# Full-height matmuls, shared memory regions with early loads, packed norms and prepared tail loads in a kernel of two attention halves

## Chip, cores, metric

The kernel runs on one core of a Trainium2 chip. The metric is the device time of one execution in microseconds (us), the median of several runs; executions of one kernel mostly agree within about 0.3%. "Span" is the length of the one execution that the profiler recorded.

The engines: PE (TensorE, matrix multiplies; PEld are its weight loads), DVE (VectorE), ACT (ScalarE), POOL (GpSimd, called PoolE in the prediction) and SP, which here only issues DMAs. "SPq" and "ACTq" in the profile are DMAs issued by SP and ACT. L459 is line 459 of the kernel file.

## The reference

One sequence of S = 2048 rows, D = 448 columns, H = 16 heads of 28. Half A is linear attention, half B is softmax attention with one shared key and value head. Outputs are the forward result of both halves, side by side, and the gradients of both inputs and all weights.

```python
# half A                                      phi(t) = where(t > 0, t + 1, exp(t)) + 1e-6
q, k, v = heads(x @ wqkv);  pq, pk = phi(q), phi(k)
kv  = einsum("bhsd,bhse->bhde", pk, v);  z = einsum("bhsd->bhd", pk)
num = einsum("bhqd,bhde->bhqe", pq, kv)
den = einsum("bhqd,bhd->bhq", pq, z)[..., None] + 1e-6
a   = join(num / den) @ wo
# half B
q = heads(x @ wq);  k = x @ wk;  v = x @ wv                   # k and v: one head of 28
p = softmax(einsum("bhqd,bkd->bhqk", q, k) * 28 ** -0.5)
b = join(einsum("bhqk,bkd->bhqd", p, v)) @ wo
out = concatenate([a, b]);  gradients = vjp(out)(grad_out)
```

D = 448 is three chunks of 128 and one of 64. A contraction over D is therefore a group of four matmuls, the last of which has only 64 rows.

## The kernel before

Cut to what the change and the argument touch; `...` marks cuts. `nc.sync` issues a DMA from SP, `nc.scalar` from ACT. Tiles of a pool with `bufs=3` share three buffers: the fourth user waits for the release of the first.

```python
DC_ROWS = [128, 128, 128, 64]
# --- half A: start and projection
xa = load_nat(cA, Ax2, "xa", nc.sync)                     # four loads
for q4 in range(4): dma_T(xaT, xa, 4 * q4, 4)             # DMA transposes, sync queue
def proj(st, off):
    ps = gen([P, D])
    for c in range(4):
        r = DC_ROWS[c]
        mm(ps[:, :], xaT[0:r, st, c, :], w3[0:r, c, off:off + D], start=(c == 0), stop=(c == 3))
    return ps
def phi(ps, dst, eng):
    E = awk.tile([P, D], F32, name="phiE")
    nc.scalar.activation(out=E[:], in_=ps[:, :], func=ACT.Exp)
    eng.tensor_scalar(out=E[:], in0=E[:], scalar1=1.0, scalar2=1e-6, op0=ALU.min, op1=ALU.add)
    nc.vector.scalar_tensor_tensor(out=dst, in0=ps[:, :], scalar=0.0, in1=E[:], op0=ALU.max, op1=ALU.add)
# --- q stage: 16 x phi(proj(st, 0), pq[...], nc.gpsimd), then the denominators
for q4 in range(4):
    ...                                                   # den = pq^T @ Zm, rden = 1 / den on DVE
    for s in range(4):
        nc.vector.tensor_scalar(out=wq_n[...], in0=pq[...], ...)
        nc.gpsimd.tensor_tensor(out=wd, in0=wd, in1=rb, op=ALU.mult)      # group "wdq" of the profile
        nc.vector.tensor_tensor(out=pv, in0=pv, in1=rb, op=ALU.mult)
...
# --- A's last stage: gradient of A's x
for st in range(NS):                                      # NS = 16 row blocks
    ps = gen([P, D])
    for tT_, w_ in [(gqT, wqT), (pkT, VWT), (gkT, wkT)]:
        for k in range(4):
            mm(ps[:, :], tT_[0:DC_ROWS[k], st, k, :], w_[0:DC_ROWS[k], k, :], ...)
    ot = awk.tile([P, D], BF16, name="osb")               # one of three buffers
    nc.any.tensor_copy(out=ot[:], in_=ps[:, :])           # ACT, here
    nc.scalar.dma_start(out1[st * P:(st + 1) * P, :], ot[:])
pa.close()                                                # all of A's memory is given back
# --- half B begins with its loads, on the sync queue
...
# --- norms: softmax is shifted by |q| * max|k|, one row per head in qT
for g in range(4):
    for qc in range(NQC):
        qs = bwk.tile([P, 512], F32, name="qsq")
        nc.vector.tensor_tensor(out=qs[:], in0=qT_B[g][...], in1=qT_B[g][...], op=ALU.mult)
        mm(ps[:, :], bsel[:, :], qs[:, :])
        for j in range(4):
            nc.scalar.activation(out=qT_B[g][32 * j:32 * j + 1, ...], in_=ps[32 * j:32 * j + 1, :],
                                 func=ACT.Sqrt, scale=kmax2_bc[32 * j:32 * j + 1, 0:1])
# --- core: 540 hand-ordered steps, not changed
# --- tail: weights, x and grad_out of B are loaded again; woB_pr in 16 loads, wqB_pad in pieces of 28 columns
woB_pr = load_wo_padrows(t4, B_wo, "woB_pr2")
wqB_pad = load_w_pad(t4, B_wq, 0, "wqB_pad2")
```

## Time and profile before

1429.03 us, median of three runs (1428.99 to 1429.32). The recorded execution has a span of 1425.0 us.

The first view is the table of windows. Each line is a stretch of the span in us, its length, the busy time of each engine with the number of instructions, the granted share of TensorE's full clock, the mean busy share of the DMA engines and what they moved. The stretches are: the q stage, A's last stage, the wait for B's loads, the norms, the steady part of the core, the wait for the tail's loads.

```profile
core 0: us, PE busy (x) PEld busy (x) DVE busy (x) ACT busy (x) POOL busy (x), PEclk, DMA share, GB/s
55.10:120.90 65.80, 54.57 (x267) 23.23 (x266) 40.96 (x74) 13.21 (x25) 47.24 (x32) 0.77 0.45 76
...
250.00:297.50 47.50, 46.37 (x193) 14.52 (x192) 1.15 (x3) 9.38 (x18) 0.00 (x0) 1.00 0.14 45
297.50:336.40 38.90, 6.62 (x49) 4.83 (x49) 6.66 (x44) 0.00 (x0) 7.84 (x16) 0.52 0.93 177
...
410.00:464.20 54.20, 31.84 (x38) 8.39 (x39) 15.42 (x22) 44.69 (x65) 0.00 (x0) 0.58 0.00 0
490.00:1305.40 815.40, 788.88 (x13334) 290.60 (x13327) 734.17 (x1336) 781.08 (x1561) 643.76 (x699) 0.99 1.05 174
1305.40:1340.90 35.50, 6.66 (x85) 3.40 (x84) 2.67 (x12) 3.40 (x8) 3.75 (x7) 0.60 0.81 187
```

No single engine bounds the kernel: each stretch has its own limit. PE bounds A's last stage, the DMAs the two waits, ACT the norms. The core is full on PE and ACT and is not touched.

The second view is the timeline of one group of four matmuls in A's last stage (start in us, busy us, engine, line, operation, shapes, count; in brackets the idle time before and what ended it). A weight load of 64 rows (256.42) is followed by the next group's first load and matmul only 0.29 us later (256.71), where full loads let matmuls start 0.19 us apart; groups start 0.97 us apart (256.71, 257.68).

```profile
256.42 0.09 PEld L94 LDWEIGHTS <-pqpT 64*128 64x128 bf16 x1 [0.37 <-issue]
256.71 0.30 PEld L94 LDWEIGHTS <-pq 128*128 128x128 bf16 x3 [0.20 <-issue]
256.71 1.04 PE L94 MATMUL agen<-KO,pq 128*128 128x448 bf16 x4
...
257.68 1.03 PE L94 MATMUL agen<-ga,gaT 128*128 128x448 bf16 x4
```

The timeline of the norms and of the core's entry: sixteen activations of one row of 512 cost 11.08 us, 0.69 each, and there are 64.

```profile
419.81 11.08 ACT L685 ACTIVATE qT_B_2018<-ps_qn,kmax_bc 1x512 bf16<-1x512 f32 x16 [0.19 <-PE ps_qn L94]
...
464.95 1.28 ACT L756 ACT_TABLE_LOAD   x1 [0.78 <-ACT qT_B_2021 L685]
466.25 0.60 ACT L756 ACTIVATE eT<-sps 128x512 bf16<-128x512 f32 x1
```

POOL's waits in the q stage (engine, line and tile, what it waited for, us in total, times, longest). With 47.24 of 65.8 us busy, POOL is idle almost only in these waits.

```profile
POOL phiE L338 <- ACT phiE L337: 9.9, 2, 5.7
POOL wdq L431 <- DVE rden L423: 6.0, 2, 4.7
```

### The profile page before, as it was taken

Reading aid. Unit: us, or ns where it says so; the run is one execution under the profiler, and the core shown is the slowest. Engines: PE = TensorE matmul, PEld = TensorE weight load, DVE = VectorE, ACT = ScalarE, POOL = GpSimd, SP = SyncE. Lnnn points to the kernel's source line nnn. Section 1 sums busy time; section 2 is a strip of 40 time slices with the busy share of each in tenths; the row PEclk is TensorE's granted clock in tenths of the full one; section 3 lists DMA queues with packets and bytes.
Section 4 is the critical chain, followed back from the end, with each engine's and each line's share of the span. In section 5 each row is a group of like instructions: output and inputs, shape, how many; then the busy total and the mean of one; then the engine's idle time right before and its main releaser. Section 6 shows DMA issues by size and latency. Waiting matters only on the chain. (4 is left out here: it accounts for less than half of the span.)

```text
span 1425.0 us, 39198 instructions
## 1 busy us (share of the span) xinstructions
PE 1261.8 (89%) x15698; PEld 473.9 (33%) x15706; DVE 896.3 (63%) x1707; ACT 961.8 (67%) x1880; POOL 768.4 (54%) x828
## 2 busy tenths in 40 slices
PE   3989979946985999999999999999999999997499
PEld 1333333311321233333333333333333333332353
DVE  1558520010131389899898998889989998886210
ACT  1321201202449899999999999999999999993123
POOL 5363070020300277778777777777777787776000
PEclk9979978967985589999999999999999999999599
DMA  9435813156200899999999998999999999994511
GB/s 250 87 58 106 166 26 67 47 126 106 67 23 0 155 159 168 176 185 168 184 190 168 187 183 164 184 185 177 179 188 160 191 187 172 194 168 134 89 52 64
DMA packets 675878, 197.33 MB, mean 138 GB/s; under 512 B 640464, under 2 KB 671152, under 8 KB 675696
## 3 DMA queue, kind: packets, MB, share of 16 engines
q1 hardware_dynamic: 665840, 186.07, 75.7%
q10 hardware_dynamic: 9728, 8.72, 2.0%
q8 instruction: 123, 2.02, 0.5%
q14 instruction: 59, 0.48, 0.1%
q0 software_dynamic: 128, 0.05, 0.0%
HBM read 24.81 MB, written 13.99 MB: 27 GB/s over the span
## 5 line engine op out<-in xcount | busy, mean ns | idle before, releaser
L764 POOL TENSOR_TENSOR dsT<-cp,eT 128x512 bf16<-128x512 bf16 x512 | 590.7, 1154 | 178.7 <-ACT cp L763 139.7
L761 DVE TENSOR_TENSOR dsT<-dps,eT 128x512 bf16<-128x512 f32 x512 | 348.6, 681 | 60.7 <-PE dps L708 34.8
L877 DVE STREAM_TRANSPOSE dsx<-dsT 128x512 f32<-128x512 f32 x512 | 358.0, 699 | 1.0
L756 ACT ACTIVATE eT<-sps 128x512 bf16<-128x512 f32 x512 | 307.8, 601 | 21.6 <-PE dps L708 15.3
L763 ACT ACTIVATE cp<-dps 128x512 bf16<-128x512 f32 x512 | 305.6, 597 | 10.3 <-PE dps L708 10.2
L766 ACT ACTIVATE eT<-sps 128x512 bf16<-128x512 f32 x512 | 312.1, 610 | 0.0
L708 PE MATMUL dk_acc<-dsx,qX 32*32 32x512 bf16 x4096 | 289.7, 377 | 0.4 <-DVE dsx L877 0.4
L708 PE MATMUL dps<-doT,vT_rep 32*128 32x256 bf16 x2048 | 262.3, 274 | 7.0 <-ACT cp L763 0.4
L708 PE MATMUL oq<-eT,vaug 128*32 128x256 bf16 x2048 | 218.1, 283 | 0.6
L708 PE MATMUL oq<-dsT,kn 128*32 128x256 bf16 x2048 | 204.0, 280 | 0.3
L708 PEld LDWEIGHTS <-kT_rep 32*128 32x128 bf16 x2048 | 90.6, 91 | 194.9 <-issue 157.1
L708 PEld LDWEIGHTS <-vaug 128*32 128x32 bf16 x2048 | 68.0, 94 | 189.9 <-issue 189.3
L708 PEld LDWEIGHTS <-qX 32*32 32x32 bf16 x4096 | 70.3, 89 | 93.4 <-issue 52.5
L708 PEld LDWEIGHTS <-vT_rep 32*128 32x128 bf16 x2048 | 85.9, 91 | 20.6 <-issue 19.9
L708 PE MATMUL dv_acc<-eN,don 128*32 128x512 bf16 x1024 | 86.7, 387 | 0.0
L708 PE MATMUL sps<-qT_B_2018,kT_rep 32*128 32x256 bf16 x512 | 65.5, 291 | 11.5 <-ACT qT_B_2021 L685 9.0
L708 PE MATMUL sps<-qT_B_2019,kT_rep 32*128 32x256 bf16 x512 | 65.4, 286 | 0.9 <-ACT eT L766 0.2
L794 POOL TENSOR_TENSOR don<-do_nat,rl 128x128 bf16<-128x128 bf16 x64 | 25.7, 402 | 71.0 <-DVE rl L786 71.0
L708 PE MATMUL sps<-qT_B_2021,kT_rep 32*128 32x256 bf16 x512 | 62.3, 276 | 0.8
L708 PE MATMUL sps<-qT_B_2020,kT_rep 32*128 32x256 bf16 x512 | 62.1, 276 | 0.8
L527 POOL TENSOR_SCALAR osb<-pk 128x448 bf16<-128x448 bf16 x16 | 27.3, 1706 | 65.8 <-ACT osb L511 64.6
L708 PEld LDWEIGHTS <-kn 128*32 128x32 bf16 x2048 | 58.5, 94 | 12.3 <-issue 6.4
(392 smaller groups left out, 1386.5 us busy)
## 6 DMA issues: line engine op xcount, KB each, us to landing
qX<-qn_d SPq DMA_DIRECT2D x128, 64.0 KB
out_dram<-osb ACTq DMA_DIRECT2D x44, 112.0 KB
eN<-eT SPq DMA_TRANSPOSE x256
xb_nat<-in_B_x_dram SPq DMA_DIRECT2D x2, 1792.0 KB
qn_d<-qn_sb SPq DMA_DIRECT2D x16, 128.0 KB
on_d<-onat SPq DMA_DIRECT2D x8, 256.0 KB
onat_B<-on_d SPq DMA_DIRECT2D x1, 2048.0 KB
xa<-in_A_x_dram SPq DMA_DIRECT2D x4, 448.0 KB
```

The lines of the kernel that those rows point to most:

```text
L527: nc.gpsimd.tensor_scalar(out=dph[:], in0=pk[:, st, 0:D], scalar1=-1e-6, scalar2=1.0, op0=ALU.add, op1=ALU.min)
L708: nc.tensor.matmul(out, lhsT=lhsT, rhs=rhs, start=start, stop=stop, tile_position=pos, skip_group_check=True)
L756: nc.scalar.activation(out=et[:, u % 2, 0, :], in_=sp[0][:, :], func=ACT.Exp, scale=scale)
L761: nc.vector.tensor_tensor(out=dst[:, 0, :], in0=dp[0][:, :], in1=ew[:, w % 2, 0, :], op=ALU.mult)
L763: nc.scalar.activation(out=cp[:, :], in_=dp[1][:, :], func=ACT.Copy)
L764: nc.gpsimd.tensor_tensor(out=dst[:, 1, :], in0=cp[:, :], in1=ew[:, w % 2, 1, :], op=ALU.mult)
L766: nc.scalar.activation(out=et[:, u % 2, 1, :], in_=sp[1][:, :], func=ACT.Exp, scale=scale)
L794: nc.gpsimd.tensor_tensor(out=dn[:], in0=dnv, in1=r_[:].to_broadcast([P, 2, 2, 32]), op=ALU.mult)
L877: nc.vector.transpose(out=dsx[b][:, tp, :, :, :].rearrange("p h t c -> p (h t c)").bitcast(F32), in_=dsT[y][:, :, :].rearrange("p h c -> p ...
```

## The change

Its intent has four parts. Matmuls outside the core get full 128-row operands, padded with zeros. A and B share three large memory regions, so that B's loads and transposes can be issued inside A. The norms pack 16 heads into one 16-row sum. The tail loads prepared weights and uses DMA transposes. Along with this the start loads x in eight pieces on two queues and transposes it on PE, the denominators move between the q projections, and all of A's stores move from ACT's queue to SP's. The diff is cut to its core.

```diff
-            for c in range(4):
-                r = DC_ROWS[c]
-                mm(ps[:, :], xaT[0:r, st, c, :], w3[0:r, c, off:off + D], ...)
+            for c in range(4):
+                mm(ps[:, :], xaT[:, st, c, :], w3[:, c, off:off + D], ...)      # likewise in all of A and B-pre
...
+    R1 = reg.tile([P, 4, S], BF16, name="R1")          # A: tT, gqn;  B: qT
+    R2 = reg.tile([P, NS, 512], BF16, name="R2")       # A: xaT;      B: do_nat
+    R3 = reg.tile([P, 4, 1408], BF16, name="R3")       # A: w3;       B: kT, vT, vaug, kn
...
+        qs = [nc.sync, nc.scalar]
+        for i in range(8):
+            qs[i % 2].dma_start(xa[:, 2 * i:2 * i + 2, 0:D], ...)
+        def xT(st): ...                                # PE transposes in place of dma_T(xaT, xa, ...)
...
+        qproj(0) ... qproj(1) ... den(0); qproj(2) ... den(1); qproj(3); den(2)      # den(3) in A's loop
...
+        xb = pk                                        # inside A: pk is free after gkn
+        load_nat(xb, Bx2, nc.sync)
...                                                     # loads of B's wq, wk, wv, wo and their spreading
+        for q4 in range(4): dma_T(xbT, xb, 4 * q4, 4)
+        ...                                            # woTp, wo_d, gb, wqTt, wqT_d, all on the sync queue
         for st in range(NS):                           # A's last stage
...
-            nc.scalar.dma_start(out1[st * P:(st + 1) * P, :], ot[:])
+            nc.sync.dma_start(out1[st * P:(st + 1) * P, :], ot[:])
...
+        for qc in range(NQC):
+            pn = gen([P, 512])
+            for g in range(4):
+                ...                                    # qT[:, g, ...] by projection, sq = qT * qT in bf16
+                mm(pn[:, :], bsel[:, g, :], sq[:, :], start=(g == 0), stop=(g == 3))
+            nc.scalar.activation(out=shift[:, ...], in_=pn[0:H, :], func=ACT.Sqrt, scale=kmax2[:, 0:1])
+        for g in range(4): nc.sync.dma_start_transpose(qn[:, :, g * P:(g + 1) * P], qT[:, g, :])
+        for h in range(H): nc.sync.dma_start(qT[32 * j:32 * j + 1, g, :], shift[h:h + 1, :])
+        nc.sync.dma_start(qn_d[:, :]..., qn[:, :, :])
...
+        for w in range(2):                             # last in B-pre: wk, wv transposed for the tail
+            wt = awk.tile([P, 512], BF16, name="osb")[:, 0:D]
+            for c in range(4): nc.sync.dma_start_transpose(wt[...], rep[0:r, w, c, :])
+            nc.sync.dma_start(wkvT_d[32 * w:32 * w + 32, :], wt[0:32, :])
```

## The prediction

> **What bounds the kernel now** (busy time per window). Half A runs to 297.5 us. PE waits for B's loads until 336.4 (busy 6.6 of 38.9). B's projections last to 410 (PE busy 72 of 74), norms to 464 (ACT busy 45 of 54, clock 0.58). The core lasts 841 us, ScalarE busy 781 of its last 815. PE then waits for reloads until 1341; the tail ends at 1425. The change touches everything but the core, 584 us. In the new order PE, VectorE and ScalarE run the core's instructions in the same order: 841 again, plus or minus 5.
>
> **Padding.** In the timeline full 128-row matmuls start 0.19 us apart. A 64-row load is not hidden: into and out of it the step is 0.29. A group of four costs 0.96 instead of 0.76. The Trainium skill (TensorE: Matmul & The Clock Gate, Part 2) says loads are pulled ahead if row groups do not conflict or the background buffer takes them; this trace agrees only for full loads. A's last stage (48 groups) falls from 47.5 to 37; B's projections lose 24 times 0.2 and, as natural-layout q becomes DMA transposes, 16 groups of 1.06.
>
> **Stage by stage**
> - Start: the first matmul (22.8) waits for A's x, whole, and its DMA transposes. Smaller loads, two queues, PE transposes: about 8. PE step 1.73 becomes 1.9. Worth 11.
> - q stage (57 to 121): PoolE is the bottleneck, 16 x 1.71 + 16 x 1.28 = 48 us, spread over 63. The denominators move into it. Worth 15.
> - A's loop: 2.96 becomes 2.6 per row block. Worth 7.
> - Rest of A: VW stays PoolE-bound (16 x 1.7). Padding worth 15, 10 of it in the last stage. A ends near 250.
> - B's load wait, 39: gone, hidden behind A's last stage.
> - B's projections and norms, 128: PE work about 47. The 64 one-row square roots of 0.69 (44 us) become 4. New chain on the sync queue after the last q copy: 4 transposes (2.7 each), 16 one-row shift writes (0.5), a 2 MB write (10), 8 small transposes (1.3), two small writes. The first exp waits for the release of A's pool, therefore for all these: 36 us after q. Core starts 64 after A ends, near 315 instead of 464.
> - Tail: 119.5 from the core's end. The reload stays: 3.9 MB before gwo at 187 GB/s (the rate there now) is 21 us, then 2.7 MB and 8 transposes of 2.7. PE order puts out-projection behind transposes, so PE waits 10, and again for dq. PE work falls from 78 to 60. About 97. Worth 22.
>
> Sum: 150 before the core, 22 after. **Predicted 1257 us, 80% range 1228 to 1290.** Faster by over 2%: 0.97; within 2%: 0.02; slower: 0.01.
>
> **What would show it:** first matmul near 8; A's end near 250; first exp near 315, released by a DMA of the sync queue; core 841; core end to finish 97, PE waiting for DMA transposes in it; no step of 0.29 in padded stages.
>
> **What would make it wrong:** A's stores are now on the sync queue, in order behind transposes and B's loads; a blocked store fills three output buffers and stops PE (5 to 20 slower). DMA transposes slower than 2.7 at the core's entry or in the tail (10 to 25). VectorE slowed beside PoolE (0.61 became 1.36 for one multiply). New waits in the core: small.

## The result, and the profile after

1260.73 us, median of four runs (1259.38 to 1261.30), against 1429.01 of the kernel before in the same rounds. The ratio is 0.8826, with a 95% interval of 0.8810 to 0.8843. A ratio here is always the mean time of one kernel's fast runs over the mean of the other's fast runs of the same rounds, so it is not quite the ratio of the medians quoted.

The total was predicted within 4 us. The stages were not. Boundaries are read from both timelines; gains are before minus after, in us.

| stage | before | after | gain | predicted gain |
|---|---|---|---|---|
| start and k stage, to the first phi on POOL | 55.1 | 44.5 | 10.6 | 11 |
| q stage | 65.8 | 65.8 | 0 | 15 |
| A's loop | 44.9 | 35.9 | 9.0 | 7 |
| rest of A before its last stage | 84.2 | 73.4 | 10.8 | 5 |
| A's last stage | 47.5 | 49.8 | -2.3 | 10 |
| wait for B's loads | 38.9 | 0 | 38.9 | 39 |
| B's projections and norms, to the first exp | 129.9 | 69.3 | 60.6 | 63 to 64 |
| core, first exp to the end | 839.2 | 836.7 | 2.5 | 0 |
| tail | 119.5 | 84.3 | 35.2 | 22 |

The gains sum to 165.3; the two spans (1425.0 and 1259.6) differ by 165.4, the rest is rounding. The first exp came at 338.65, not near 315, and the tail took 84.3, not 97: two errors of opposite sign.

The windows after: the q stage, A's last stage, the stretch from the last q copy to the first exp, the steady part of the core, the tail, and the first 10 us of the tail:

```profile
core 0: us, PE busy (x) PEld busy (x) DVE busy (x) ACT busy (x) POOL busy (x), PEclk, DMA share, GB/s
44.50:110.30 65.80, 43.47 (x275) 21.40 (x273) 42.49 (x78) 12.19 (x23) 47.36 (x32) 0.84 0.47 77
...
219.50:269.40 49.90, 39.07 (x195) 19.49 (x193) 0.57 (x1) 8.81 (x18) 2.02 (x17) 0.86 0.79 185
...
300.50:338.70 38.20, 21.31 (x211) 11.30 (x213) 3.06 (x6) 13.66 (x23) 0.17 (x1) 0.84 0.57 120
364.00:1175.30 811.30, 785.46 (x13318) 289.71 (x13314) 732.15 (x1332) 779.29 (x1558) 642.19 (x697) 1.00 1.08 176
1175.30:1259.60 84.30, 66.96 (x412) 32.26 (x416) 12.38 (x22) 17.04 (x35) 3.16 (x3) 0.89 0.73 184
1175.30:1185.30 10.00, 4.63 (x80) 2.55 (x81) 3.65 (x8) 2.73 (x5) 3.16 (x3) 0.90 0.93 301
```

In A's last stage PE's work fell from 46.4 to 39.1 us, as intended, but the stage did not shrink. The timeline there shows why:

```profile
238.41 5.37 SPq L101 DMA_TRANSPOSE kv<-K_154  x4
243.88 1.50 SPq L460 DMA_DIRECT2D out_dram<-osb  x3
...
245.87 1.49 ACT L459 CAST osb<-agen 128x448 bf16<-128x448 f32 x3 [17.04 <-DMA out_dram<-osb]
246.45 1.65 PE L79 MATMUL agen<-KO,pq 128*128 128x448 bf16 x4 [10.83 <-ACT osb L459]
...
247.90 1.70 PE L79 MATMUL agen<-ga,pqpT 128*128 128x448 bf16 x4
...
252.70 0.92 PE L79 MATMUL agen<-ga,gaT 128*128 128x448 bf16 x4
...
253.45 0.73 PE L79 MATMUL agen<-KO,pq 128*128 128x448 bf16 x3
```

Read it backwards. PE stood still for 10.83 us until ACT copied a result out of PSUM (L459). ACT had waited 17.04 us for a store that had to free one of three output buffers. The stage's first three stores (L460) were not issued before 243.88, behind transposes for B on the same queue, although the stage began at 219.56. Afterwards PE runs at half speed for about 4 us: groups start 1.45 to 1.5 us apart (246.45, 247.90, 249.39) instead of 0.76 (252.70, 253.45). The Trainium skill (TensorE: Matmul & The Clock Gate, Part 1) says that an idle window of about 3.4 us halves PE's clock, and a busy one restores it; this trace agrees: after the 10.83 us without work the granted clock was 0.50 from 246.45 to 250.88, and the steps are full again from 251.94 on.

POOL's waits in the q stage after: the sum (3.7 + 12.0 = 15.7) is that of before (9.9 + 6.0 = 15.9).

```profile
POOL phiE L205 <- ACT phiE L204: 3.7, 1, 3.7
POOL wdq L281 <- DVE rden L273: 12.0, 4, 5.0
```

The core's entry. The last q copy is done at 300.47. Four transposes (10.46 us) and 16 shift rows (10.08 us) follow on the sync queue, then:

```profile
321.21 0.58 SPq L521 DMA_DIRECT2D qn_d<-pk  x1
321.89 13.97 SPq L538 DMA_TRANSPOSE osb<-K_155  x8
...
336.03 1.39 SPq L539 DMA_DIRECT2D wkvT_d<-osb  x2
337.36 1.28 ACT L624 ACT_TABLE_LOAD   x1 [14.74 <-DMA osb<-K_155]
...
338.65 0.60 ACT L624 ACTIVATE eT<-sps 128x512 bf16<-128x512 f32 x1
```

ACT waits for the eight small transposes, which the core itself does not need: they hold memory that the core's first tiles reuse. In the tail the gradient of wo starts 10.0 us after the core's end (1175.33), where the prediction had counted 21:

```profile
1185.34 4.98 PE L79 MATMUL pacc<-gb_24528,onat_B 128*128 128x448 bf16 x13 [2.87 <-DMA gb_24528<-in_grad_out_dram]
```

### The profile page after: what moved, and what is told of

It reads as the page before. It is cut to its first block, busy times and chain, and to the rows that moved or that the text cites. A ratio compares the mean times of both kernels' runs of the same rounds, so it can differ in the third digit from the quotient of the medians.

```text
span 1259.6 us, 38409 instructions
## 1 busy us (share of the span) xinstructions
PE 1136.0 (90%) x15382; PEld 457.1 (36%) x15388; DVE 876.8 (70%) x1601; ACT 904.9 (72%) x1788; POOL 781.1 (62%) x861
## 4 chain that ended last, share of the span: by engine, by line
PE 56%; ACT 20%; issue 8%; POOL 5%; DVE 4%; SPq 4%; DMA 2%; ACTq 0%; POOLq 0%; DVEq 0%
PE dk_acc L576 15%; PE oq L576 10%; PE agen L79 10%; ACT eT L634 9%; ACT cp L631 9%; PE sps L576 7%; PE dps L576 5%; PE dv_acc L576 2%; PE aacc L79 2%; POOL osb L383 2%; PE pgen L79 2%; POOL phiE L205 2%; PE sps L690 1%; SPq L87 1%; PE pacc L79 1%
## 5 line engine op out<-in xcount | busy, mean ns | idle before, releaser
L576 PEld LDWEIGHTS <-R_65 32*128 32x128 bf16 (+1 forms) x8192 | 174.3, 93 | 420.8 <-issue 375.7
L631 ACT ACTIVATE cp<-dps 128x512 bf16<-128x512 f32 x512 | 305.4, 596 | 10.2 <-PE dps L576 10.1
L576 PE MATMUL sps<-R_63,R_65 32*128 32x256 bf16 x2048 | 254.0, 281 | 19.9 <-ACT eT L624 16.2
L576 PE MATMUL dps<-doT,R_65 32*128 32x256 bf16 x2048 | 261.2, 273 | 7.0 <-DVE dsT L629 0.3
L576 PE MATMUL oq<-eT,R_65 128*32 128x256 bf16 x2048 | 218.1, 283 | 0.5
L576 PE MATMUL oq<-dsT,R_65 128*32 128x256 bf16 x2048 | 203.7, 279 | 0.3 <-ACT R_63 L739 0.2
L736 DVE COPY oTs<-oq 64x256 f32<-64x256 f32 x64 | 26.7, 417 | 59.3 <-ACT eT L624 39.8
L662 POOL TENSOR_TENSOR don<-R_64,rl 128x128 bf16<-128x128 bf16 x64 | 25.8, 403 | 42.5 <-DMA eN<-eT 42.5
L205 POOL TENSOR_SCALAR phiE<-phiE 128x448 f32<-128x448 f32 x16 | 27.3, 1706 | 20.5 <-DVE zrow L230 15.7
L79 PE MATMUL agen<-R_65,R_64 128*128 128x448 bf16 x128 | 33.2, 405 | 6.2 <-ACT R_64 L192 4.5
L576 PEld LDWEIGHTS <-don 128*32 128x32 bf16 x1024 | 34.8, 98 | 0.5
```

The lines of the kernel that those rows point to most:

```text
L79: nc.tensor.matmul(out_ap, lhsT=lhsT, rhs=rhs, start=start, stop=stop, tile_position=(0, 0))
L576: nc.tensor.matmul(out, lhsT=lhsT, rhs=rhs, start=start, stop=stop, tile_position=pos, skip_group_check=True)
L631: nc.scalar.activation(out=cp[:, :], in_=dp[1][:, :], func=ACT.Copy)
L662: nc.gpsimd.tensor_tensor(out=dn[:], in0=dnv, in1=r_[:].to_broadcast([P, 2, 2, 32]), op=ALU.mult)
L736: nc.vector.tensor_copy(out=oTs[v // 8][:, :], in_=oq[0:64, 0:256])
```

## The experiments

Twelve kernels were run, each timed in three rounds, each with the right result. Times are medians; "after" is 1260.73. Each group shared the runs of the kernel before (medians 1426.8 to 1429.5). The kernel after the change was timed in other rounds than these runs, so a difference to it in us is rough: by the ratios, experiments 1 and 2 and the two runs of experiment 3 give -8.3, -13.4, +4.7 and -2.7 us instead of the -8.9, -14.8, +3.2 and -3.1 below. The interval of the change is 0.8810 to 0.8843; where a run's interval overlaps it, as in both runs of experiment 3, the time decides nothing. Each run has one trace.

| run | us | ratio to before, 95% |
|---|---|---|
| stores of A's last stage on ACT's queue | 1251.88 | 0.8768 (0.8750 to 0.8787) |
| q's phi on VectorE | 1245.95 | 0.8732 (0.8713 to 0.8751) |
| wk and wv transposes early | 1263.94 | 0.8859 (0.8838 to 0.8880) |
| the same, own buffers | 1257.65 | 0.8807 (0.8790 to 0.8823) |
| padding undone | 1287.28 | 0.9014 (0.8992 to 0.9035) |
| before with compact norms alone | 1400.33 | 0.9807 (0.9793 to 0.9822) |
| before with a wide load of wq in the tail | 1424.20 | 0.9982 (0.9958 to 1.0005) |
| B's loads later in the program | 1255.33 | 0.8792 (0.8775 to 0.8810) |
| x of B forced late, stores on ACT's queue | 1258.51 | 0.8810 (0.8795 to 0.8824) |
| four repairs | 1234.48 | 0.8643 (0.8628 to 0.8659) |
| four repairs, tail's stores on ACT's queue | 1235.96 | 0.8646 (0.8623 to 0.8669) |
| four repairs, transposes kept out of the stores | 1230.78 | 0.8621 (0.8592 to 0.8650) |

### 1. Which queue holds the stores

```diff
-            nc.sync.dma_start(out1[st * P:(st + 1) * P, :], ot[:])
+            nc.scalar.dma_start(out1[st * P:(st + 1) * P, :], ot[:])
```

> Edit: after the change, with the sixteen stores of A's last stage back on the ScalarE queue, as they were before the change. Theory (blocked store queue): the stall of 10.8 us of PE at 246, released by an eviction that waited for a store, is made by the sync queue, on which the stores stand behind B's transposes and loads; the last stage, 49.6 us, falls to 36 to 39 us and the time by 9 to 13 us, to 1248 to 1252. Rival (DMA engines are full there, whoever issues): the stall moves or stays, the last stage stays above 46 us and the time falls by less than 4 us.

Measured: 1251.88, 8.9 us less. The window of the last stage in this run:

```profile
core 0: us, PE busy (x) PEld busy (x) DVE busy (x) ACT busy (x) POOL busy (x), PEclk, DMA share, GB/s
220.80:258.90 38.10, 36.60 (x195) 18.83 (x193) 0.57 (x1) 8.76 (x18) 2.02 (x17) 1.00 1.10 226
```

The stage takes 38.0 us from its first group (220.87) to the first projection of B (258.85), at full clock, and the DMA engines move 226 GB/s instead of 185. The engines were not full; the queue was blocked. The rival falls. The predicted length of the stage, 37, is nearly reached once the store queue is repaired.

The Trainium skill (DMA: Bandwidth & Descriptors, Issuing engines are not separate DMA queues) says that starting DMAs from several engines only saves the time of issuing, which is usually small. Here it was not small. The issue of the sixteen stores themselves takes 0.34 to 0.49 us each. But on the shared queue the first three stood behind other DMAs, whose records fill 14.2 of the 14.9 us from 229.01 to 243.88, and moving the stores bought 8.9 us. The skill's page Perfetto Trace Analysis (DMA Optimizations, separating input and output engines) gives the advice that fits, and this run agrees with it.

### 2. What bounds the q stage

```diff
-                phi(proj(st, 0), pq[:, st, 0:D], nc.gpsimd)
+                phi(proj(st, 0), pq[:, st, 0:D], nc.vector)
```

> Edit: after the change, with the min-add step of phi in the q stage on VectorE instead of PoolE (16 instructions of 1.71 us leave PoolE). Theory (the q stage is bound by PoolE): the stage, 42.9 to 110.3, gets 12 to 20 us shorter, the time falls to 1241 to 1249. Rival (the stage is bound by the chain of DMA transposes, denominators and reciprocals, or by VectorE): the stage keeps 63 us or more and the time falls by less than 5 us, or rises.

Measured: 1245.95, 14.8 us less. The stage from the first phi to the loop:

```profile
core 0: us, PE busy (x) PEld busy (x) DVE busy (x) ACT busy (x) POOL busy (x), PEclk, DMA share, GB/s
45.00:96.90 51.90, 39.52 (x276) 20.27 (x275) 46.89 (x94) 12.20 (x25) 20.08 (x16) 0.93 0.56 97
```

POOL lost 27.3 us of work, VectorE gained 4.4, and the stage shrank by 13.9. So POOL's work was on the path, and the theory stands; but half of the 27 us was not returned, so POOL was not the only limit. The same instruction (min and add on 128x448 fp32) takes 1.71 us on POOL and 0.39 on VectorE (in the k stage before; in this run 0.38 at the median and up to 1.13). The Trainium skill (GPSIMD Engine Reference, 4.1 Engine selection) calls GpSimd roughly line-rate for one input; here it is 4.3 times slower than VectorE.

### 3. What holds the core's first exp

The block that transposes wk and wv was moved from the end of B's preparation to its start.

```diff
+        for w in range(2): ...                 # moved here, ahead of B's projections
         for qc in range(NQC):
             for w, dst in [(0, kT), (1, vT)]:
...
-        for w in range(2): ...                 # was last in phase_B_pre
```

> Edit: after the change, with the eight small transposes and two writes of B's wk and wv (for the tail) issued before B's projections instead of after the 2 MB write of q. Theory (the first exp waits for the release of A's pool, which these transposes hold): the first exp moves from 338.7 to between 323 and 329 and the time falls by 8 to 14 us, to 1247 to 1253. Rival (the first exp waits for the write of q, the shift rows or ScalarE's table load, whichever comes last anyway): the first exp stays after 334 and the time falls by less than 4 us.

Measured: 1263.94, 3.2 us more, which is not clear of noise. The theory seemed to fall. The timeline shows what was overlooked:

```profile
272.28 10.05 SPq L478 DMA_TRANSPOSE osb<-K  x8
...
284.16 0.41 DVE L496 TENSOR_TENSOR osb<-R 32x512 bf16<-32x512 bf16 x1 [9.87 <-DMA wkvT_d<-osb]
...
338.01 1.28 ACT L624 ACT_TABLE_LOAD   x1 [6.46 <-DMA qn_d<-pk]
```

The moved transposes took two of the three buffers named osb, and the k norms, which use the same buffers, waited 9.87 us for them. q came 8.9 us later (first transpose of q at 309.40 instead of 300.47), while the way from there to the first exp shrank from 38.2 to 29.9 us. The next run took the buffers out of the picture.

```diff
-            wt = awk.tile([P, 512], BF16, name="osb")[:, 0:D]
+            wt = pqr[:, 5 + w, 0:D]
```

> Edit: as the run before that moved the eight small transposes of wk and wv ahead of B's projections, but with a place of their own (free columns of pq) in place of two of the three shared output buffers. There the k norms waited for those buffers, q came 9 us later (first transpose of q at 309.4 against 300.5), and the way from there to the first exp shrank from 38.2 to 29.9 us. Theory (the late transposes hold the release of A's pool): q comes again near 300, the first exp near 330, the time falls by 6 to 10 us, to 1251 to 1255. Rival (something else delayed q in that run, or the norms gain only because they came late): the first exp stays after 336 and the time within 3 us of 1261.

Measured: 1257.65, only 3.1 us less, which is not clear of noise. From the first transpose of q to the first exp it took 30.1 us, 8.1 less than after the change, and the wait is now that of the 2 MB write of q (6.67 us). But q again came late, at 307.03. In this run the scheduler put the eight transposes (11.0 us of the sync queue, from 258.23) in front of A's last stores, into the very queue of experiment 1. The last stage was not longer for it (50.0 us), but A's last copies came late, and PE then stood 2.86 us for them (277.18). Another 2.8 us of the delay were there before the stage began (222.36 instead of 219.56); this edit does not explain them. So the transposes do hold the core's entry, for 8 us; moving them on that queue gives part of it back. The run's expectation of 330 for the first exp was missed (337.14).

### 4. What padding is worth

Data, buffers, loads and order stay as after the change; only the fourth chunk's rows are cut.

```diff
+    def kr(c, r=64):
+        return slice(0, r if c == 3 else P)
-                mm(ps[:, :], xaT[:, st, c, :], w3[:, c, off:off + D], ...)
+                mm(ps[:, :], xaT[kr(c), st, c, :], w3[kr(c), c, off:off + D], ...)
...                                             # likewise in ten more contractions
```

> Edit: the padding alone undone in the kernel after the change: the fourth chunk of every contraction outside the core reads its 64 (80) rows instead of 128; data, buffers, loads and order stay. Theory (a 64-row weight load is not hidden, 0.2 us for each group of four matmuls): A's last stage gets 8 to 11 us longer, A's loop 4 to 7, B's projections and dO 6 to 9, the k and q stages under 4 together, as PoolE and phi set them; the time rises by 18 to 28 us, to 1279 to 1289. Rival (the groups are hidden behind evictions, stores and the stall): the time rises by less than 8 us.

Measured: 1287.28, 26.6 us more, in the upper part of the expected range. Against the trace after the change the points of the timeline shift by 2.3 us at the start of the q stage, 10.3 at the end of A's loop, 14.2 at the start of A's last stage, 20.4 at A's end, 23.6 at the first exp and 25.9 at the finish. The steps between groups are back at 0.97 (286.85, 287.82) instead of 0.76:

```profile
286.85 1.03 PE L79 MATMUL agen<-KO,pq 128*128 128x448 bf16 x4
...
287.82 1.03 PE L79 MATMUL agen<-ga,pqpT 128*128 128x448 bf16 x4
```

The last stage grew by 6.2 us only (9.6 would be 48 groups of 0.2): slower groups waited less at the blocked stores, 6.72 instead of 10.83 us. Computing with zeros pays here. The Trainium skill (TensorE: Matmul & The Clock Gate, LDWEIGHTS) says that the time of a weight load does not depend on its rows; the trace before agrees (0.09 us for 64 rows, 0.10 for 128). The cost is that the short load is not hidden behind the running matmul.

### 5. The compact norms alone, in the kernel before

```diff
-                    for j in range(4):
-                        nc.scalar.activation(out=qT_B[g][32 * j:32 * j + 1, ...], ..., func=ACT.Sqrt, ...)
+                    mm(pn[:, :], bsel[:, g, :], qs[:, :], start=(g == 0), stop=(g == 3))   # bf16 squares
+                nc.scalar.activation(out=shift[:, ...], in_=pn[:, :], func=ACT.Sqrt, scale=kmax2_bc[0:H, 0:1])
+            for h in range(H):
+                nc.sync.dma_start(qT_B[g][32 * j:32 * j + 1, :], shift[h:h + 1, :])
```

> Edit: the kernel before, with the compact norms alone: sixteen heads packed into one 16-row sum (bf16 squares), four square roots of 16x512 instead of 64 of one row, sixteen row writes of the shift. Theory (the 64 one-row activations of 0.69 us set that stretch): the stretch from the first square root to the first exp, 418.3 to 466.3, falls to 22 to 30 us, and the time by 18 to 26 us, to 1403 to 1411; the ratio to the kernel before is 0.982 to 0.988. Rival (the stretch is set by the fp32 matmuls at half clock, the table loads and the pool's release): the time falls by less than 8 us.

Measured: 1400.33, 27.5 us less than the 1427.79 of its rounds, slightly more than expected. The first exp moved from 466.25 to 437.69.

```profile
424.36 0.68 ACT L686 ACTIVATE shift<-ps_qn,kmax_bc 16x512 bf16<-16x512 f32 x1 [1.10 <-PE ps_qn L94]
425.07 10.10 SPq L690 DMA_DIRECT2D qT_B<-shift  x16
...
436.40 1.28 ACT L759 ACT_TABLE_LOAD   x1 [11.36 <-DMA qT_B<-shift]
```

One activation of 16 rows costs 0.68 us, as much as one of a single row. The theory stands; the 64 small activations set that stretch. The run also turned the fp32 squares and their matmuls into bf16, so it does not separate the two by itself; the trace before does, as ACT runs its activations there without gaps (16 in 11.08 us) and PE waits for them. What remains is the 16 row writes, for which ACT waits 11.36 us; the prediction had counted them as a link of the new chain.

### 6. What the tail waited for before

```diff
-            wqB_pad = load_w_pad(t4, B_wq, 0, "wqB_pad2")          # DMA writes pieces of 28 columns, 56 bytes
+            wqn = load_w_nat(t4, B_wq, D, "wq2n")                  # whole rows
+            ...                                                    # four copies on VectorE spread them
```

> Edit: the kernel before, with the tail's wq loaded in whole rows of 896 bytes and spread to the padded layout by four copies on VectorE, instead of by DMAs with packets of 56 bytes; bytes and order stay. Theory (the tail's wait consists of 17 us of bulk at 340 GB/s and then of slow narrow packets at 50 to 77 GB/s, so the 187 GB/s of the prediction is a mean over two things): the PE transposes of wq end near 1334 instead of 1339.5, the stretch from the core's end to the finish is 4 to 8 us shorter. Rival (bytes set the wait): it stays within 2 us of 119.6.

Measured: 1424.20. The interval of the ratio, 0.9958 to 1.0005, contains 1, so the time alone decides nothing. The profiles, one of each kernel, say more: from the core's end to the finish it is 114.2 us (1306.35 to 1420.5) instead of 119.5, and the transposes of wq end about 1336.4 instead of 1339.5. The windows of the kernel before, three microseconds each, show what the mean of 187 GB/s hid:

```profile
core 0: us, PE busy (x) PEld busy (x) DVE busy (x) ACT busy (x) POOL busy (x), PEclk, DMA share, GB/s
...
1313.00:1316.00 3.00, 0.00 (x0) 0.00 (x0) 0.00 (x0) 0.00 (x0) 0.00 (x0) 0.50 1.10 340
...
1331.00:1334.00 3.00, 0.58 (x4) 0.35 (x4) 0.00 (x0) 0.00 (x0) 0.00 (x0) 0.50 1.28 80
1334.00:1337.00 3.00, 0.60 (x4) 0.34 (x4) 0.00 (x0) 0.00 (x0) 0.00 (x0) 0.50 1.29 43
```

The large loads run at 340 GB/s. Then the pieces of 56 bytes keep the DMA engines at least as busy (1.28 and 1.29) at 43 to 80. Between the two, from 1325 to 1328, lies a third phase: SP issues the last of the sixteen loads of wo, and the DMA engines are mostly idle (share 0.17, 44 GB/s). This run left that phase as it was (0.16, 37 GB/s). The Trainium skill (DMA: Bandwidth & Descriptors, Specifications) asks for 512 bytes or more for full rate, and the trace agrees. After the change nothing narrow stands before the first matmul of wo's gradient, and it starts 10.0 us after the core's end. In these 10 us the DMAs moved 301 GB/s, about 3.0 of the 3.9 MB: grad_out now comes in four pieces, and the first matmuls need only the first.

### 7. Is hiding B's loads worth the whole wait?

All of B's loads and transposes were moved behind A's last stage in the program.

```diff
-        xb = pk;  load_nat(xb, Bx2, nc.sync);  ...;  dma_T(xbT, ...);  ...;  load_nat(gb, ...);  ...
         for st in range(NS): ...               # A's last stage
+        load_nat(xb, Bx2, nc.sync);  ...;  dma_T(xbT, ...);  ...;  load_nat(gb, ...);  ...
```

> Edit: after the change, with all loads and transposes for B issued after A's last stage instead of inside A; regions, padding, norms and tail stay. Theory (the early issue hides the wait for B's loads and pays for it with the blocked stores): A's last stage loses its stall of 10.8 us and half-clock steps, 49.6 becomes 36 to 40; behind it PE waits 22 to 35 us for x of B and its transposes; the time rises by 12 to 24 us, to 1273 to 1285. Rival (hiding the loads was worth the whole wait of before, 39 us, and the stall has nothing to do with them): the last stage stays above 46 us and the time rises by 30 us or more.

Measured: 1255.33, 5.4 us less; both theories expected more time. The run did not do what it was made for. The trace shows that the scheduler issued the loads where they had been (x of B at 170.99 and its first transposes at 216.35, after the change at 170.13 and 216.41), and that only the order of stores and transposes on the sync queue changed: the stage's first store came at 226.52 instead of 243.88. Its last stage took 38.8 us. So this supports experiment 1 a second time, and says nothing on hiding. To force x late, it was given memory that A reads to its end:

```diff
-        xb = pk
+        xb = pq                                # read by A's last stage
             ...
-            nc.sync.dma_start(out1[st * P:(st + 1) * P, :], ot[:])
+            nc.scalar.dma_start(out1[st * P:(st + 1) * P, :], ot[:])
```

> Edit: after the change, with the stores of A's last stage on the ScalarE queue (so that the stall is out of the picture), and x of B loaded not into pk, which is free early, but into pq, which A's last stage reads to its end; so x and its four transposes can only be finished behind it, whatever order the scheduler chooses. To be compared with the run with the stores on the ScalarE queue alone (1251.9). Theory (the early region for x hides only the load of x and its transposes, of which the last quarter and four transposes of 2.7 us would be exposed): PE waits 6 to 15 us at the border of A and B and the time is 5 to 15 us above that run, 1257 to 1267. Rival (x was the whole of the wait of 39 us before the change): 30 us or more above it. Third: nothing, if the transposes run in the shadow of other work of PE: less than 3 us.

Measured: 1258.51, 6.6 us above the run with the stores alone on ACT's queue (1251.88).

```profile
265.48 3.15 PE L79 MATMUL agen<-wdq,K 128*128 128x512 bf16 x7 [6.29 <-DMA wdq<-pq]
```

PE waits 6.29 us for the first transpose of x (258.72), which on the sync queue stands behind the load of the last quarter of x (257.71). That is what the early place of x is worth, given that grad_out, the weights and the first quarters of x are still loaded inside A. The rest of the 39 us was not taken apart further.

### 8. The repairs together

Stores on ACT's queue, q's phi on VectorE, the wk and wv transposes early in their own place, and the 2 MB write of q ahead of most shift rows:

> Edit: after the change with four repairs together: stores of A's last stage on the ScalarE queue, phi's min-add of the q stage on VectorE, the transposes of wk and wv before B's projections in a place of their own, and the 2 MB write of q ahead of the shift rows. If the stalls are independent (measured alone: 9, 15 and 3; the last came with A's last stage 3 to 5 us longer, because its transposes stood before the blocked stores, which the first repair ends, so 7 for it here, and 3 to 6 for the order of the write), the time falls by 30 to 38 us, to 1223 to 1231; A ends near 245, the first exp near 300. Rival (the wk and wv repair gains nothing beside the store repair, or the moved transposes and stores collide on the DMA engines): the time falls by 20 to 26 us only, to 1235 to 1241.

Measured: 1234.48, 26.2 us less than after the change: short of the theory (30 to 38) and just outside the rival's range (20 to 26). The last stage took 44.0 us instead of 38.0; two of ACT's copies waited 9.42 and 3.60 us, by the profile for DMA transposes. The 9.42 us ended before the moved transposes were issued (240.51) and are put down to those of grad_out; the 3.60 us, and 2.15 us of the next copy, to the moved ones. From the first transpose of q to the first exp it took 28.2 us, so putting the write first gained 2 us.

A further run also moved 32 of the tail's stores to ACT's queue:

```diff
-                nc.sync.dma_start(out_8[h * DH:(h + 1) * DH, :], ...)
+                nc.scalar.dma_start(out_8[h * DH:(h + 1) * DH, :], ...)
-            nc.sync.dma_start(out4[st * P:(st + 1) * P, :], ot[:])
+            nc.scalar.dma_start(out4[st * P:(st + 1) * P, :], ot[:])
```

> Edit: as the kernel with the four repairs, and in the tail the sixteen small stores of the wo gradient and the sixteen of the x gradient on the ScalarE queue too, as the sync queue there stands behind four transposes of dq until 1217. Theory (the same blocked stores stop PE in the tail, about 10 of 17 us busy between 1200 and 1217): core end to finish falls from 84 to between 74 and 80 us, the time is 4 to 10 us below the kernel with the four repairs. Rival (PE waits there for the transposes themselves and the DMA engines are full): within 2 us of it.

Measured: 1235.96, the same within noise. In the tail, then, the place of the stores is not what stops PE; the rival stands.

In the last run the transposes of wk and wv write to the last two blocks of pq, so that they cannot run beside A's stores:

```diff
-            wt = pqr[:, 5 + w, 0:D]
+            wt = pqr[:, 14 + w, 0:D]
```

> Edit: as the kernel with the four repairs, but the transposed wk and wv go into the last two blocks of pq, which A's last stage reads to its end, so that the scheduler cannot put these eight transposes between that stage's stores. In the kernel with four repairs the last stage took 44.0 us (206.6 to 250.6) against 38.7 with the store repair alone, with evictions waiting 9.4 and 3.6 us beside DMA transposes. Theory (transposes that run beside the stores slow the stores, on whichever queue these are): the last stage takes 38 to 41 us, the first exp comes 3 to 6 us earlier and the time is 1228 to 1232. Rival (the collision is with the transposes of grad_out, which stay): the last stage stays above 43 us and the time within 2 us of 1234.5.

Measured: 1230.78 (1229.18 to 1235.37). The last stage is back at 38.1 us, and the first exp came at 305.94 instead of 310.83. The time is 3.7 us below that of the four repairs, but the two were in different rounds and the intervals of their ratios overlap (0.8592 to 0.8650 and 0.8628 to 0.8659). The stage supports the mechanism; a gain in time is not shown. The stage had begun 4.3 us earlier (202.31 instead of 206.62), before anything that the edit touches, and of the 5.8 us by which it was shorter 5.0 were lost again behind it, where the first transpose of q came 37.1 us after A's end instead of 32.1. This is the version with the lowest median: 30 us below the kernel after the change, 14% below the kernel before.

## Why the prediction was right and where it was wrong

The time, 1260.73 us, lies within the predicted range and 4 us from the predicted 1257. It was right as a sum of large terms that were right; that it is as near as 4 us is luck, as errors cancelled.

**Right, in size too.** The start gained 10.6 (predicted 11). The wait for B's loads was gone (39). The core stayed (836.7 for 841 plus or minus 5). B's projections and norms took 69.3 (predicted 64), and the first exp was released by a DMA of the sync queue, as said; experiment 3 shows that the eight transposes were the last link, and experiment 5 that the packed norms are worth 27.5 us by themselves. Padding: experiment 4 puts the whole of it at 26.6 us. A's loop gained 9.0 (predicted 7).

**Wrong: "PoolE is the bottleneck ... The denominators move into it. Worth 15."** The first half was right, as experiment 2 shows: taking POOL's phi away gives 14.8 us. The conclusion was wrong. The 15 us between POOL's 48 us of work and the 63 us of the stage were counted as slack that interleaving would close. But they were waits of POOL for other engines, and the new order put the same work of PE in front of them. The longest before was for the exp of a projection (77.51), which PE computed behind the products KO and KOT (69.15 to 77.51):

```profile
77.51 3.93 PE L94 MATMUL agen<-w_103,xaT 128*128 128x448 bf16 x16
...
79.20 14.19 POOL L338 TENSOR_SCALAR phiE<-phiE 128x448 f32<-128x448 f32 x8 [5.73 <-ACT phiE L337]
```

The longest after was for denominators, which PE computed (80.42) behind the same products (72.28 to 80.42):

```profile
80.42 0.56 PE L79 MATMUL agen<-Zm,R_63 128*128 128x16 bf16 x16
...
81.94 5.21 POOL L281 TENSOR_TENSOR wdq<-wdq,rden 128x448 bf16<-128x448 bf16 x4 [5.03 <-DVE rden L273]
```

Only for the last quarter's denominators (99.31) does the profile show PE waiting for that quarter's transposes. Interleaving changed the single waits (9.9 + 6.0 became 3.7 + 12.0) and not their sum. The new order has the same 32 instructions on the same engine and the same idle sum. That PE's order made these waits is read from the timelines; no run moved the products.

**Wrong: "Padding worth 15, 10 of it in the last stage. A ends near 250."** The padding is there (PE's work fell by 7.3 us, the stage reaches 38.0 with free stores), but the stage grew by 2.3 because of the blocked stores. The prediction named this as a risk, "a blocked store fills three output buffers and stops PE (5 to 20 slower)", and left it out of the sum. It cost 11.8 us of that stage and 8.9 of the time. With the q stage's 15 it explains why A ended at 269 instead of 250, partly made good by the stretch before the last stage, which gained 10.8 instead of 5; what else than padding (about 4 us, experiment 4) shortened that stretch was not isolated.

**Wrong in the other direction: "3.9 MB before gwo at 187 GB/s ... is 21 us".** It took 10.0. The 187 GB/s was the mean of a window that held a phase at 340 GB/s, a phase of idle DMA engines and a phase of narrow pieces at 43 to 80, and the change had just removed the last two; besides, only about 3.0 of the 3.9 MB had moved when the gradient of wo started. This term, 11 us, is most of the 13 us by which the tail came out better. The waits behind it were somewhat shorter than the 10 us predicted: PE was busy 10.0 of 17 us between 1200 and 1217.

**Core entry.** 36 us were predicted from the last q copy to the first exp, 38.2 were measured. The last link was read correctly from the diff. In the chain, errors cancelled: the shift rows held the sync queue for 10.1 us instead of 8 and the eight transposes for 14.0 instead of 10.4, while the 2 MB write, counted with 10, held it for 0.6 and ran beside the transposes.

In the sum: the first exp 24 us late, the core 4 us and the tail 13 us short, which leaves 7 us of 1253 (315 + 841 + 97); the prediction's 1257 came from subtracting rounded gains.

## What to carry to other kernels

An engine's idle share is not slack until one knows what each gap waits for: reorder only if the new order puts other work in the gap, and otherwise take work off that engine. In these traces the DMAs of one queue were issued one after the other, so stores that free a small ring of buffers must not share it with loads and transposes issued early, and every moved DMA must be checked for which buffers and which queue place it takes. Before a mean rate is carried into a new kernel, split its window: a rate averaged over wide and narrow transfers fits neither.

## What the Trainium skill lacked or had wrong

- DMA: Bandwidth & Descriptors (Issuing engines are not separate DMA queues): it says that a second issuing engine saves only issue time, usually small. Moving sixteen stores to another queue gained 8.9 us and raised the rate of the stage from 185 to 226 GB/s. That section does not say that a DMA also stands behind the issue of everything in front of it on its queue (14.2 of 14.9 us here).
- TensorE: Matmul & The Clock Gate (Part 2): it lacks the price of mixed heights. Among 128-row loads one of 64 rows cost about 0.10 us going in and 0.10 coming out (groups 0.97 apart instead of 0.76), 26.6 us in this kernel when padding was undone.
- GPSIMD Engine Reference (4.1 Engine selection): one-input work is called roughly line-rate; min and add on 128x448 fp32 took 1.71 us on GpSimd and 0.39 on VectorE.
- ScalarE: Activation LUTs (What ACT_TABLE_LOAD costs): a switch of the table is given as about 2.7 us, 1.28 for the load and 1.38 for a drain. The load took 1.28 us here, but a drain does not show: at the first square root after the change one activation ended at 289.18, the load started at 289.20 and the next activation at 290.49, 1.31 us in all.
